# Stores of converted weight blocks moved from SyncE's DMA queue to ScalarE's, in an attention kernel followed by two feed-forward layers

## Chip, cores and metric

One core of one Trainium2 chip runs the whole program. The metric is the device time of one execution in microseconds (us); the time of a kernel is the median of its runs. A granted TensorE clock of 1.0 in a row is the 2.4 GHz level, 0.5 would be 1.2 GHz.

## What is computed

Pooled attention over 4 batches and 8 heads (q is averaged over pairs of neighbouring rows, so 576 query rows meet 1152 keys of 64 elements), then two feed-forward layers of 512 to 2048 to 512 on all 2304 rows, the first with a leaky ReLU, the second with an ELU.

```
q_pool = q.reshape(B, H, S // 2, 2, D).mean(axis=3)
scores = scale * q_pool @ k.T
attn   = softmax(scores)
x      = (attn @ v), heads side by side            # 2304 x 512
h = x @ w_in;  g = maximum(0.01 * h, h);           x = g @ w_out
h = x @ w_in2; g = where(h > 0, h, exp(min(h, 0)) - 1); out = g @ w_out2
```

q, k and v are float32. [...]

## The kernel before

**Matmuls.** Each float32 operand is split into a high part (rounded to the PE's float32r) and a low rest, and products are summed over two or three pairs of parts. The helper `psplit` (L261) records both steps: the rounding (L266 on ScalarE, called ACT below) and the subtraction (L272 on GpSimd, called POOL, or on VectorE, called DVE).

**Order of the work.** Nothing is issued where it is written. `prog.add` records an operation with its engine, an assumed cost, a rank (the smaller, the sooner) and the tiles it reads and writes; `Program.schedule` (L86) then plays all of it through with these costs, takes on each engine the ready operation of the lowest rank, and `emit` writes the instructions out in the order of the start times that come out. That order is fixed: on the chip each engine works through its own list and waits on semaphores. SyncE (SP) has no arithmetic; it issues DMAs, and each one in its list holds back those behind it while it waits. ACT computes and issues DMAs from the same list.

**Stages.** 16 pairs of heads (4 batches with 4 pairs each) go through attention. The feed-forward layers of a batch are woven into the attention of later batches by rank: `PLAN` (L219) starts layer 1 of batch 0 at rank 36 and its layer 2 at rank 54. Each layer takes the 2048 hidden elements in 16 blocks f of 128: `up` (L623) forms one block, and after every four blocks `down` (L662) sums them into the output.

**Weights.** `load_w` (L316) fetches for block f two pieces of 128 x 512, one of w_in and one of w_out, into two of four `wr` tiles. In batch 0 they are converted there by `convert` (L276): ACT issues the load of 512 KB of float64 into one of two `cr` tiles (L294), DVE makes the high bits (L297, L300), ACT scales the low word (L303) and takes the absolute value (L305), POOL adds (L308), and DVE clears the too small ones (L310). The block in `wr` is then stored to DRAM (L333, 256 KB, from SP's queue), and batches 1 to 3 read it back from there (L328, SP) without a conversion. In every batch the block goes from `wr` through `psplit` into `wi` or `wo` (rounding on ACT, subtraction on POOL). A `wr` tile can be overwritten once its rounding, its subtraction and its store are done.

**SP's other work.** In the same list stand the loads of q, k and v (L354), which use three `raw` tiles in turn; a load waits until POOL has finished with the tile. POOL splits k (L264, L272) and adds the pairs of rows of q (L402).

The lines that matter: L333, the store; L294, the loads that ACT issues already; L354, the loads of q, k and v on SP; L297 to L310, the conversion.

Of the kernel before, what the change touches and what calls it, by code (L numbers as in the profile page):

```python
# [157 lines left out]
def kernel(  # L158
# [19 lines left out]
    nc = tc.nc  # L178
# [59 lines left out]
    def f32(ap):  # L238
        return ap.bitcast(F32)
# [4 lines left out]
    prog = Program()  # L244

    def sb(tag, shape, dt=F32, bufs=1):
        return prog.buf(tag, bufs, lambda: sp.tile(shape, dt, tag=tag, name=tag, bufs=bufs))
# [4 lines left out]
    def act(n, accum=False, sbuf=False):  # L252
        return 50 + 0.833 * n + (190 if accum else 0) + (43 if sbuf else 0)

    def dve(n, fast=False):
        return 66 + (0.52 if fast else 1.05) * n

    def pool(n):
        return 140 + 2.12 * n

    def psplit(rank, h, l, hi, lo, src, n, w, r, w_l=None, fast=True, psum=False):  # L261

        if h == "POOL":
            prog.add("POOL", 100 + 1.1 * n, rank, lambda: G.tensor_copy(out=hi(), in_=src()), w=[w], r=r)  # L264
        elif h == "ACT":
            prog.add("ACT", act(n, sbuf=not psum), rank, lambda: A.activation(out=hi(), in_=src(), func=ACTF.Copy), w=[w], r=r)  # L266
        else:
            prog.add("DVE", dve(n, fast), rank, lambda: V.tensor_copy(out=hi(), in_=src()), w=[w], r=r)  # L268
        eng = V if l == "DVE" else G
        prog.add(  # L270
            l, dve(n) if l == "DVE" else pool(n), rank,
            lambda: eng.tensor_tensor(out=lo(), in0=src(), in1=f32(hi()), op=ALU.subtract),  # L272
            w=[w_l or (w[0], "l")], r=[w] + r)
# [42 lines left out]
    def load_w(rank, layer, w_in, w_out, f):  # L316

        src = (w_in[:, f * 128:(f + 1) * 128].rearrange("(c p) f -> p c f", p=128),
               w_out[f * 128:(f + 1) * 128, :])
        rs = [sb("wr", [128, 512], F32, WRB) for _ in range(2)]  # L320
        for i, r in enumerate(rs):
            if w_in.dtype == F32:
                view = (lambda r=r: r.ap.rearrange("p (c n) -> p c n", c=DC)) if i == 0 else lambda r=r: r.ap
                prog.add("SP", 60, rank - 1.5, lambda i=i, view=view: nc.sync.dma_start(
                    out=view(), in_=src[i]), w=[r])
            elif (layer, f, i) in kept:
                kp = kept[layer, f, i]
                prog.add("SP", 60, rank - 1.5, lambda r=r, kp=kp: nc.sync.dma_start(  # L328
                    out=r.ap, in_=kp.ap), w=[r], r=[kp])
            else:  # L330
                convert(rank - CLEAD, r, src[i])
                kp = kept[layer, f, i] = Buf(lambda i=i: dram.tile([128, 512], F32, name=f"w{layer}_{f}_{i}"))
                prog.add("SP", 60, rank, lambda r=r, kp=kp: nc.sync.dma_start(out=kp.ap, in_=r.ap), w=[kp], r=[r])  # L333
        wi = sb("wi", [128, 2, DC, 128], F32R, WIB)
        wo = sb("wo", [128, 2, DM], F32R, WOB)
        psplit(rank - 0.5, WH, WL, lambda: wi[:, 0].rearrange("p c n -> p (c n)"),
               lambda: wi[:, 1].rearrange("p c n -> p (c n)"), lambda: rs[0].ap, 512, (wi, 0), [rs[0]])
        psplit(rank - 0.5, WH, WL, lambda: wo[:, 0], lambda: wo[:, 1], lambda: rs[1].ap, 512, (wo, 0), [rs[1]])
        return wi, wo


# [258 lines left out]
    def mlp(at, span, b, layer, xin, w_in, w_out, tags):  # L600
# [22 lines left out]
        def up(f):  # L623
            rank = at + step * f
            w[f] = load_w(rank - WLEAD * step, layer, w_in, w_out, f)
            wi = w[f][0]
            g[f] = sb("g", [128, 2, NQ], F32R, GB)
# [108 lines left out]
    for b, layer, at, wide in PLAN:  # L736
        tags = [(u, size[u]) for u in ("h" * HBUFS + ("t" * TB + "s" * SBUFS if wide else ""))]
        w = ((moe_w_in, moe_w_out), (moe2_w_in, moe2_w_out))[layer]
# [35 lines left out]
```

## Time and profile before

| | |
|---|---|
| median of 3 runs | 1553.42 us (1551.05 to 1557.32) |
| the profiled execution, its own time | 1551.51 us |
| its span, first to last instruction | 1549.7 us |
| PE busy | 1416.1 us, 91% |
| ACT busy | 1017.4 us, 66% |
| DVE busy | 976.6 us, 63% |
| POOL busy | 874.8 us, 56% |
| stores of converted blocks | 64, from 35.3 to 581.7 us |
| float64 loads | 64, from 0.7 to 570.0 us |

Issuing a DMA does not count as busy; in the views of the trace such instructions stand under ACTq and SPq. "Idle before" an instruction is the idle time of its engine, and behind the arrow stands what ended it. Busy shares are means over the span; the stretch up to 585 us, in which weights are converted, is a different stage from the one behind it.

### The profile page before, as it was taken

To read this page: it belongs to the slowest core of one execution; us is meant where nothing else is said; L and a number is where in the kernel's file an instruction comes from. 1 tells how busy PE (TensorE), PEld (TensorE's weight loads), DVE (VectorE), ACT (ScalarE), POOL (GpSimd) and SP (SyncE) were. 2 spreads that over 40 slices of the span, in tenths; PEclk is the share of its full clock that TensorE was granted. 3 is DMA by queue.
4 is the path that set the end of the run, shared out by engine and by line. 5 is a ranking of instruction groups with operands and counts; after the bars stand their busy time and mean duration, and the time that the engine had idled before them with its cause. 6 is when DMAs were issued, how large, how long until landed. Compare 5 with 4: busy or idle time off the path is not lost.

```text
span 1549.7 us, 28278 instructions
## 1 busy us (share of the span) xinstructions
PE 1416.1 (91%) x10288; PEld 1359.9 (88%) x10288; DVE 976.6 (63%) x2081; ACT 1017.4 (66%) x2709; POOL 874.8 (56%) x840
## 2 busy tenths in 40 slices
PE   5878898889789988999999999999999998899998
PEld 4777788878778878999999999999999998898997
DVE  6999798788977887656665556656665554124122
ACT  5888777666677776666567776666567763442553
POOL 6544355756776686454565655454565445465562
PEclk9999999999999999999999999999999999999999
DMA  4332123424433432221222222221222111222221
GB/s 137 106 121 80 39 66 128 161 85 153 137 120 131 152 124 90 75 74 63 66 69 85 79 77 63 81 78 57 67 67 63 55 55 55 92 81 70 76 82 39
DMA packets 77516, 135.53 MB, mean 87 GB/s; under 512 B 7488, under 2 KB 25920, under 8 KB 77376
## 3 DMA queue, kind: packets, MB, share of 16 engines
q1 hardware_dynamic: 55872, 100.16, 20.6%
q10 hardware_dynamic: 21504, 33.56, 6.4%
q8 instruction: 81, 1.33, 0.4%
q14 instruction: 59, 0.48, 0.1%
HBM read 112.20 MB, written 21.50 MB: 86 GB/s over the span
## 4 chain that ended last, share of the span: by engine, by line
PE 51%; ACT 7%; DVE 6%; DMA 2%; issue 2%; POOL 1%; ACTq 0%; DVEq 0%; POOLq 0%
PE h L672 16%; PE h L634 12%; PE s L457 5%; PE o L501 4%; PE t L480 4%; PE s L634 3%; PE s L672 2%; PE t L672 2%; PE t L634 2%; ACT p L468 1%; DVE xs L268 1%; PE t L378 1%; ACT t L650 1%; DVE t L655 1%; DMA cr<-in_moe_w_in_dram 1%
## 5 line engine op out<-in xcount | busy, mean ns | idle before, releaser
L672 PE MATMUL h<-g,wo 128*128 128x288 f32 x2544 | 443.8, 304 | 22.5 <-DVE t L655 7.3
L634 PE MATMUL h<-xs,wi 128*128 128x288 f32 x2520 | 422.0, 303 | 21.4 <-DVE t L655 11.4
L672 PEld LDWEIGHTS h<-g,wo 128*128 128x128 f32 x2544 | 368.4, 189 | 30.1 <-DVE t L655 9.3
L634 PEld LDWEIGHTS h<-xs,wi 128*128 128x128 f32 x2520 | 357.2, 189 | 32.1 <-DVE t L655 17.7
L266 ACT ACTIVATE pt<-t 128x384 fp32r<-128x384 f32 (+1 forms) x416 | 185.3, 457 | 134.4 <-PE t L480 116.7
L462 DVE TENSOR_REDUCE m<-s 128x1 f32<-128x384 f32 x432 | 229.1, 550 | 68.2 <-PE s L457 65.6
L272 POOL TENSOR_TENSOR wo<-wr,wo 128x512 fp32r<-128x512 f32 x128 | 166.3, 1305 | 168.0 <-ACT wo L266 154.9
L468 ACT ACTIVATE p<-s,m 128x384 f32<-128x384 f32 x432 | 249.5, 587 | 15.9 <-DVE m L464 13.6
L272 POOL TENSOR_TENSOR g<-t,g 128x288 fp32r<-128x288 f32 x256 | 216.8, 853 | 75.4 <-ACT g L266 72.6
L272 DVE TENSOR_TENSOR pt<-t,pt 128x384 fp32r<-128x384 f32 (+1 forms) x416 | 206.5, 509 | 71.8 <-ACT pt L266 70.6
L457 PE MATMUL s<-kT,qT 128*128 128x384 f32 x768 | 194.5, 356 | 26.8 <-ACT p L468 25.3
L272 POOL TENSOR_TENSOR wi<-wr,wi 128x512 fp32r<-128x512 f32 x128 | 171.0, 1336 | 72.9 <-ACT wi L266 66.7
L501 PE MATMUL o<-pt,vn 128*128 128x256 f32 (+1 forms) x1152 | 191.1, 301 | 6.4 <-DVE pt L272 5.5
L480 PE MATMUL t<-ident,p 128*128 128x128 f32 x1116 | 181.8, 275 | 15.5 <-DVE pt L272 11.2
L501 PEld LDWEIGHTS o<-pt,vn 128*128 128x128 f32 x1152 | 164.4, 189 | 10.9 <-DVE pt L272 9.4
L480 PEld LDWEIGHTS t<-ident,p 128*128 128x128 f32 x1116 | 137.1, 141 | 27.1 <-DVE pt L272 14.0
L457 PEld LDWEIGHTS s<-kT,qT 128*128 128x128 f32 x768 | 126.3, 193 | 36.3 <-ACT p L468 33.2
L266 ACT ACTIVATE wo<-wr 128x512 fp32r<-128x512 f32 x128 | 80.8, 632 | 92.0 <-PE h L672 56.6
L266 ACT ACTIVATE g<-t 128x288 fp32r<-128x288 f32 x256 | 112.4, 447 | 34.7 <-DVE t L655 21.0
L264 POOL CAST vn<-raw 128x576 fp32r<-128x576 f32 x32 | 22.3, 696 | 181.2 <-PE o L501 181.2
L685 DVE TENSOR_TENSOR acc<-h,acc 128x288 f32<-128x288 f32 x158 | 70.8, 452 | 74.8 <-PE h L672 73.8
L308 POOL TENSOR_TENSOR wr<-wr,cr 128x512 uint32<-128x512 uint32 x64 | 88.9, 1393 | 33.6 <-DVE wr L300 16.7
(106 smaller groups left out, 2025.1 us busy)
## 6 DMA issues: line engine op xcount, KB each, us to landing
wr<-w SPq DMA_DIRECT2D x192, 256.0 KB, 2.6
cr<-in_moe_w_in_dram ACTq DMA_DIRECT2D x32, 512.0 KB, 4.0
cr<-in_moe_w_out_dram ACTq DMA_DIRECT2D x32, 512.0 KB, 4.3
w<-wr SPq DMA_DIRECT2D x64, 256.0 KB, 2.5
raw<-in_k_dram SPq DMA_DIRECT2D x32, 288.0 KB, 3.1
raw<-in_v_dram SPq DMA_DIRECT2D x32, 288.0 KB, 3.0
raw<-in_q_dram SPq DMA_DIRECT2D x32, 256.0 KB, 2.6
out_dram<-cr SPq DMA_DIRECT2D x16, 256.0 KB, 2.3
```

Of the source, the lines that this page charges most:

```text
L264: prog.add("POOL", 100 + 1.1 * n, rank, lambda: G.tensor_copy(out=hi(), in_=src()), w=[w], r=r)
L266: prog.add("ACT", act(n, sbuf=not psum), rank, lambda: A.activation(out=hi(), in_=src(), func=ACTF.Copy), w=[w], r=r)
L272: lambda: eng.tensor_tensor(out=lo(), in0=src(), in1=f32(hi()), op=ALU.subtract),
L308: prog.add("POOL", pool(CW), rank, lambda t=t, r=r: G.tensor_tensor(out=t(), in0=t(), in1=r[:, :, 0], op=ALU.add), w=[(dst, n)], r=[(dst, ...
L457: PE.matmul(out=st[:, 0:384], lhsT=qa(a), rhs=kT[:, 384 * c:384 * c + 384], start=(i == 0), stop=(i == len(seq) - 1))
L462: prog.add("DVE", dve(384), rank - LR, lambda st=st, c=c: V.tensor_reduce(out=m[:, c:c + 1], in_=st[:, 0:384], axis=AX.X, op=ALU.max), w=[ ...
L468: prog.add("ACT", act(384, True), rank - LE, lambda c=c: A.activation(out=p[:, 384 * c:384 * c + 384], in_=banks[c][:, 0:384], func=ACTF.E ...
L480: PE.transpose(out=t[:, i, :], in_=p[:, (3 * c + i) * 128:(3 * c + i + 1) * 128], identity=ident)
L501: PE.matmul(out=o[:, 0:n], lhsT=vn[:, c, :], rhs=pt[th][:, a, c % 3, :], start=(c == 3 * ORDER[0] and a == 0), stop=(c == 3 * ORDER[2] + 2 ...
L634: PE.matmul(out=h[:, 0:HB], lhsT=wi[:, a, c, :], rhs=xs[c][:, e, cols], start=(c == 0 and a == 0 and e == 0), stop=(c == DC - 1 and a == 1))
L672: PE.matmul(out=y[:, 0:HB], lhsT=w[f][1][:, a, d * 128:(d + 1) * 128], rhs=g[f][:, e, cols], start=(f % FC == 0 and a == 0 and e == 0), st ...
L685: prog.add("DVE", dve(HB), rank - HURRY, lambda y=y, a_=a_, cols=cols: V.tensor_tensor(out=a_[:, cols], in0=y[:, 0:HB], in1=a_[:, cols], o ...
```

## The change

The two stores of a block are no longer recorded for SP inside the loop that converts, but collected, and recorded for ACT after both roundings, with a rank 0.1 behind that of the roundings, an assumed cost of 80 ns, and an assumed 3000 ns until the data has landed. The line of the store is L342 in the changed kernel, and lines behind it are five higher.

```diff
         rs = [sb("wr", [128, 512], F32, WRB) for _ in range(2)]
+        stores = []
         for i, r in enumerate(rs):
...
                 convert(rank - CLEAD, r, src[i])
                 kp = kept[layer, f, i] = Buf(lambda i=i: dram.tile([128, 512], F32, name=f"w{layer}_{f}_{i}"))
-                prog.add("SP", 60, rank, lambda r=r, kp=kp: nc.sync.dma_start(out=kp.ap, in_=r.ap), w=[kp], r=[r])
+                stores.append((kp, r))
...
         psplit(rank - 0.5, WH, WL, lambda: wo[:, 0], lambda: wo[:, 1], lambda: rs[1].ap, 512, (wo, 0), [rs[1]])
+        for kp, r in stores:
+            prog.add("ACT", 80, rank - 0.4, lambda r=r, kp=kp: nc.scalar.dma_start(out=kp.ap, in_=r.ap), w=[kp], r=[r],
+                     late=3000)
         return wi, wo
```

What this makes of the lists is seen at three places. In a name, `w_11_0` is the store of block 11's piece of w_in, `w_11_1` that of w_out; `cr` loads are the float64 blocks. A bracket names the semaphores that an instruction waits on: DMAHW the completion of an earlier DMA, the others an engine's progress.

ACT, the conversion of blocks 11 and 12 of layer 1, before:

```order
L266 ACTIVATE pt<-t 128x3x128 [waits PE_49]
L294 DMA cr<-in_moe_w_in_dram 128x4x256 [waits DMAHW7_49,DVE_49]
L468 ACTIVATE p,sum<-s,m 128x384
L266 ACTIVATE pt<-t 128x3x128 [waits PE_49]
L423 ACTIVATE rem_73<-t 128x2x64 [waits PE_49]
L423 ACTIVATE rem_75<-t 128x2x64
L294 DMA cr<-in_moe_w_out_dram 128x1024 [waits DMAHW3_49,DVE_49,Activation_49]
L303 ACTIVATE cr<-cr 128x512 [waits DMAHW7_49]
```

and in the changed kernel:

```order
L266 ACTIVATE pt<-t 128x3x128 [waits PE_49]
L294 DMA cr<-in_moe_w_in_dram 128x4x256 [waits DVE_49]
L342 DMA w_11_0_3975<-wr 128x512 [waits DMAHW1_49]
L266 ACTIVATE pt<-t 128x3x128 [waits PE_49]
L294 DMA cr<-in_moe_w_out_dram 128x1024 [waits DVE_49,Activation_49]
L342 DMA w_11_1_4000<-wr 128x512 [waits DMAHW4_49]
L473 ACTIVATE p,sum<-s,m 128x384 [waits DVE_49]
```

A store now stands right behind a float64 load; none of the 64 waits on DVE itself, because an instruction ahead of it on ACT has waited for that already. Of the 64, 34 stand behind an ACTIVATE and 30 behind another DMA issue; 36 stand ahead of the rounding of their own block, which comes later in the list.

ACT, blocks 6 and 7 of layer 1, before:

```order
L294 DMA cr<-in_moe_w_in_dram 128x4x256
L266 ACTIVATE pt<-t 128x3x128
L682 ACTIVATE acc<-h 128x288
L266 ACTIVATE pt<-t 128x3x128
L294 DMA cr<-in_moe_w_out_dram 128x1024
L266 ACTIVATE pt<-t 128x3x128
```

and in the changed kernel:

```order
L294 DMA cr<-in_moe_w_in_dram 128x4x256
L266 ACTIVATE pt<-t 128x3x128
L687 ACTIVATE acc<-h 128x288
L266 ACTIVATE pt<-t 128x3x128
L342 DMA w_6_0_3191<-wr 128x512
L342 DMA w_6_1_3193<-wr 128x512
L342 DMA w_7_0_3195<-wr 128x512
L294 DMA cr<-in_moe_w_out_dram 128x1024
L266 ACTIVATE pt<-t 128x3x128
L342 DMA w_7_1_3214<-wr 128x512
```

Four stores have come together here, three of them ahead of a float64 load: the longest such run. From here to block 12 of layer 2 the order of PE, DVE and POOL differs too.

SP, around the end of layer 1's conversion, before:

```order
L333 DMA w_14_1_4543<-wr 128x512
L354 DMA raw<-in_v_dram 128x576
L333 DMA w_15_0_4634<-wr 128x512
L354 DMA raw<-in_k_dram 128x576
L354 DMA raw<-in_q_dram 128x512
L333 DMA w_15_1_4672<-wr 128x512
```

and in the changed kernel:

```order
L359 DMA raw<-in_v_dram 128x576
L359 DMA raw<-in_k_dram 128x576
L359 DMA raw<-in_q_dram 128x512
L359 DMA raw<-in_v_dram 128x576
L359 DMA raw<-in_k_dram 128x576
```

SP's list has lost the stores, and the loads of q, k and v follow each other in the same order as before.

## Rows read from the trace of the kernel before

**Rows 1.** The page: span, and busy time of the engines.

```profile
span 1549.7 us, 28278 instructions
PE 1416.1 (91%) x10288; PEld 1359.9 (88%) x10288; DVE 976.6 (63%) x2081; ACT 1017.4 (66%) x2709; POOL 874.8 (56%) x840
```

**Rows 2.** Busy time by stretch: length, PE, PEld, DVE, ACT, POOL, clock, DMA.

```profile
35.00:215.00 180.00, 148.46 (x1042) 135.66 (x1041) 162.43 (x372) 149.25 (x426) 81.53 (x78) 0.98 0.27 84
215.00:585.00 370.00, 320.16 (x2209) 295.61 (x2209) 305.47 (x573) 267.13 (x673) 252.55 (x214) 0.99 0.39 131
585.00:1550.00 965.00, 927.75 (x6930) 911.55 (x6929) 487.07 (x1096) 581.42 (x1562) 518.03 (x517) 1.00 0.22 70
```

**Rows 3.** The same view, the fullest and the emptiest 50 us while weights are converted.

```profile
250.00:300.00 50.00, 45.97 (x328) 43.59 (x327) 37.47 (x75) 38.36 (x98) 34.32 (x30) 0.97 0.35 118
400.00:450.00 50.00, 39.56 (x277) 36.69 (x276) 45.90 (x87) 33.59 (x84) 34.82 (x31) 0.99 0.35 116
```

**Rows 4.** The chain that ended last, 473 to 586 us, shares by line.

```profile
by line: DMA cr<-in_moe_w_in_dram 11.4%; DMA cr<-in_moe_w_out_dram 11.1%; issue 9.2%; DVE wr L297 7.1%; PE h L672 6.0%; DVE wr L310 5.9%; DVE wr L300 5.8%; PE h L634 5.8%; DVE m L462 4.2%; ACT p L468 3.9%; DVE t L655 2.9%; ACT cr L303 2.8%;
```

**Rows 5.** The stores on SP: waits (us, times, longest) and issue (ns min/median/max).

```profile
SPq L333 <- DVE wr L310: 318.8, 56, 13.9
L333 SPq DMA_DIRECT2D w<-wr x64: 319/321/337, 35.3 to 581.7; - x64
```

**Rows 6.** The float64 loads on ACT's queue: ns min/median/max, first and last start.

```profile
L294 ACTq EVENT_SEMAPHORE  x51: 17/17/2407, 32.9 to 567.8; - x51
L294 ACTq DMA_DIRECT2D cr<-in_moe_w_in_dram x32: 385/406/462, 0.7 to 567.9; - x32
L294 ACTq DMA_DIRECT2D cr<-in_moe_w_out_dram x32: 334/342/523, 1.2 to 570.0; - x32
```

**Rows 7.** ACT in order of time, around a single load: start us, us.

```profile
85.28 0.33 ACT L266 ACTIVATE pt<-h 128x192 fp32r<-128x192 f32 x1
85.37 0.33 ACTq L294 DMA_DIRECT2D cr<-in_moe_w_out_dram  x1
85.51 0.33 ACT L266 ACTIVATE pt<-h 128x192 fp32r<-128x192 f32 x1
```

**Rows 8.** ACT in order of time, around a pair of loads.

```profile
58.93 0.39 ACTq L294 DMA_DIRECT2D cr<-in_moe_w_in_dram  x1
59.43 0.44 ACTq L294 DMA_DIRECT2D cr<-in_moe_w_out_dram  x1
59.92 0.49 ACT L266 ACTIVATE pt<-t 128x384 fp32r<-128x384 f32 x1 [0.51 <-PE s L457]
```

**Rows 9.** ACT in order of time, a load issued at the end of an ACTIVATE.

```profile
534.66 0.39 ACTq L294 DMA_DIRECT2D cr<-in_moe_w_in_dram  x1
535.10 0.58 ACT L468 ACTIVATE p<-s,m 128x384 f32<-128x384 f32 x1 [0.41 <-DVE pt L272]
```

**Rows 10.** POOL's waits from 215 to 585 us: us, times, longest.

```profile
POOL qs L402 <- DMA raw<-in_q_dram: 13.5, 5, 3.7
```

**Rows 11.** Around 363 us in order of time: POOL, then SP, then DVE.

```profile
358.76 1.60 POOL L272 TENSOR_TENSOR kn<-raw,kn 128x576 fp32r<-128x576 f32 x1
...
367.80 0.77 POOL L402 TENSOR_TENSOR qs<-raw 128x256 f32<-128x256 f32 x1 [3.19 <-DMA raw<-in_q_dram]
368.54 1.30 POOL L308 TENSOR_TENSOR wr<-wr,cr 128x512 uint32<-128x512 uint32 x1
...
362.24 0.32 SPq L333 DMA_DIRECT2D w<-wr  x1
362.65 0.38 SPq L354 DMA_DIRECT2D raw<-in_k_dram  x1
363.14 0.39 SPq L354 DMA_DIRECT2D raw<-in_q_dram  x1
...
367.30 0.68 DVE L300 SCALAR_TENSOR_TENSOR wr<-cr,wr 128x512 uint32<-128x512 uint32 x1
...
370.02 0.68 DVE L310 SCALAR_TENSOR_TENSOR wr<-cr,wr 128x512 f32<-128x512 f32 x1
```

## Prediction, made before the changed kernel was run

> **What bounds the kernel now.** I began with the busy times of the page. PE is busy 1416.1 of 1549.7 us [rows 1], so all that a faster order could win is some 130 us of PE's idle time. The busy times by stretch say where that lies [rows 2]. From 585 us on, PE is busy 927.75 of 965 us, 96%: that part is bound by PE, holds no store, and keeps its order of instructions, so I carry it over as it is. From 215 to 585 us PE is busy 320.16 of 370 us, so 50 us are idle; from 35 to 215 us 148.46 of 180, so 32 us. The 64 stores run from 35.3 to 581.7 us [rows 5], in just these stretches. No engine is full in the longer one: DVE has 305.47 of 370 us, ACT 267.13, POOL 252.55. So the end is set by a chain that changes engines, and I read that next. Between 473 and 586 us the chain that ended last goes through the float64 loads (11.4 + 11.1%), the three DVE steps of the conversion (7.1 + 5.8 + 5.9%), and ACT's exponentials and scaling of low words (3.9 + 2.8%) [rows 4]. The stores are not named in it. What they can change is therefore how soon ACT gets through its list, since ACT issues the float64 loads, and how soon SP gets through its own.
>
> **Off SP.** SP loses 64 issues of 321 ns, and with them the waits in front of them: 318.8 us in 56 waits for L310 [rows 5]. SP computes nothing, so this counts only through the loads of q, k and v that stand behind a waiting store. Who is late because of them? From 215 to 585 us POOL waited five times for a q load, 13.5 us together [rows 10]. One of these places in full [rows 11]: POOL was done with the k tile at 358.76 + 1.60 = 360.36 us, but SP still held a store until 362.24, and issued k at 362.65 and q at 363.14. Without the store k could go at about 360.4, so q would land 2.3 us sooner and most of POOL's 3.19 us is gone. But what POOL does next, the addition L308 at 368.54, also needs L300 on DVE, which ended at 367.30 + 0.68 = 367.98. So L308 starts 0.56 us sooner at most, and DVE, which had other work until 370.02, need not notice. Bounds for this term: nothing, and all 13.5 us. I take **-1 us**, near the lower end, because this place, which is the row nearest to the question, gives at most 0.56 us and there are five of its kind.
>
> At this point the page "DMA: Bandwidth & Descriptors" of the Trainium skill (section "Issuing engines are not separate DMA queues") speaks against the change: all queues end on the same DMA engines, and issuing from another engine saves only issue time. By it this term would be 0 instead of -1. The 2.3 us of the place above disagree a little: what is saved there is a place in a list, not issue time.
>
> **Onto ACT: the issue.** Two kinds of issue on this queue last 406 and 342 ns [rows 6], and what one costs depends on what stands ahead of it. Behind an ACTIVATE, with nothing to wait for, it can be free: the load at 85.37 us was issued during the ACTIVATE from 85.28, and the next began at 85.51, before the issue was over [rows 7]. Of 25 loads that began to be issued before the ACTIVATE ahead had ended and have no other issue next to them, 18 read like this one and seven leave 2.8 us idle together; the one at 534.66, with 0.41, is of these [rows 9]. That is 2.8 / 25, about 0.1 us each. Behind another issue there is no cover: in the pair at 58.93 and 59.43 us the second left ACT idle for 0.51 us [rows 8], and I take 0.45, between its own 0.44 and that. With 34 stores of the first kind and 30 of the second the sum is 34 x 0.1 + 30 x 0.45 = 17 us of idle ACT. Bounds: 0, if all are covered, and 64 x 0.45 = 29 us.
>
> The page "Advanced Engine Details and Errata" (section "Sequencer and Instruction Queues") says that a sequencer pushes instructions ahead into a queue, eight deep on ScalarE, so that an issue runs beside them. By it the second kind could be covered as well and the 17 us would shrink to some 3; the 0.51 us of the pair go against it, and I go by them.
>
> How much of 17 us is on the path? In the chain the float64 loads and the two named ACT steps make up 11.4 + 11.1 + 3.9 + 2.8 = 29% [rows 4]; the loads come out of ACT's list, so they are late when it is. Not each of these pieces has a store ahead of it, so I take a quarter: **+4 us**. The bounds are 0 and the whole 29.
>
> **Onto ACT: the waits.** None of the stores waits for DVE; 44 of the 64 wait for an earlier DMA with the same completion semaphore, 22 of these for one of SP's. The nearest such DMA stands 14 ACT instructions earlier, and 14 at about half a microsecond are 7 us, longer than a transfer takes to land. So **0 us**. The bound above: the float64 loads carry the same kind of wait, and the longest time that this queue stood in one was 2407 ns while the median is 17 [rows 6]; a few of that length would stay below 10 us. Behind a store that waits stand the exponentials and the next float64 load, and for these wait the PE and the conversion.
>
> **Moved.** With the stores on ACT the planner brings other instructions out in another order between block 6 of layer 1 and block 12 of layer 2, about 245 to 580 us. Counted in the order of PE, blocks 4 to 11 of layer 1 start up to 27 matmuls of attention later, blocks 4 to 9 of layer 2 up to 17 earlier, and from block 12 on nothing differs. A `wr` tile is held until its store has landed, but between a store and the scaling for the next block in its tile stand at least 8 ACT instructions, nearly always over 15, so no new wait is expected there. The same work in a slightly other order has no sign that I can read: **0 us**. For the size, the fullest and the emptiest 50 us of this stage differ by 45.97 - 39.56 = 6.4 us of PE [rows 3], so I allow 6.4 us either way.
>
> **Sum.** -1 + 4 + 0 + 0 = +3 us. The profiled execution took 1551.5 us, which gives 1554.5; it lies 1.9 us below the median of the three runs (1553.4), so in terms of a median the forecast is **1556 us**, +0.2%. By a measurement of this kernel about 0.5%, 7.8 us, can be told from no change, so this is "no difference". Its own range is 1546 to 1561.
>
> **Rivals.**
> *Slower: ACT becomes the bound of the conversion.* Then the 17 us are not a quarter but wholly on the path. For it: from 35 to 215 us ACT is busy 149.25 of 180 us, 83%, without counting issues, and in the longer stretch each float64 load passes through its list. Against it: 9% of the chain is idle "issue" and most of the rest is DVE, DMA and PE [rows 4]. It gives 1551.5 + 17 - 1 + 1.9 = 1569, with the upper bound of 29 even 1581. It decides from 8 us on, a good half of the 17. Chance 0.22.
> *Faster: SP's list was the brake.* If each q load were in time and the stores were covered, 13.5 us of POOL's waiting would come back: 1551.5 - 13.5 + 1.9 = 1540. For it: the wait at 367.80 us stands right ahead of a conversion step on POOL [rows 11]. Against it: DVE's next step of that conversion began at 370.02, behind other work. Chance 0.15.
> *The other order decides.* It adds or takes 6.4 us: 1550 or 1563, the latter over the bound of 7.8 us, the former beyond it only if a term above ends at its low end too. What speaks for it is that two stretches of the same work differ by so much [rows 3], and against it that the list of PE is the same again from block 12 of layer 2 on. Chance 0.10, of which I count half as faster and half as slower.
> *The change doesn't do what it says.* The stores stand behind the roundings by rank only, and 36 come ahead of their own. But as none waits for DVE, this changes no time, and I leave it within the forecast.
>
> **How the numbers follow.** Forecast 0.53; slower 0.22 + 0.05 = 0.27; faster 0.15 + 0.05 = 0.20. The range that holds 8 in 10 reaches from 1542, which cuts off the deeper half of the faster case, to 1571, which holds the slower case at its 17 us and leaves out its upper bound.
>
> **What would show it.** Right: stores of about 0.35 us under ACTq, ACT's busy time unchanged at 1017 us, PE's busy time from 215 to 585 us the same within a few us, POOL's wait for q loads down from 13.5 us to under 6, and the stretch after 585 us unchanged in length. Wrong to the slow side: long waits under ACTq at L342, or a chain with ACT ahead of DVE. Wrong to the fast side: conversion ending well before 582 us and PE's idle time between 35 and 585 us well below the 82 us of now.

## The result: 15 us slower, and the profile after

The changed kernel takes 1567.57 us (median of 4 runs, 1565.01 to 1568.13) where the kernel before takes 1552.43 beside it (4 runs): ratio 1.0089, 95% interval 1.0063 to 1.0114. Timed once more, beside the hybrids below, it took 1564.91 us (6 runs, 1561.95 to 1566.78), ratio 1.0069 (1.0051 to 1.0087). So it is slower by 11 to 15 us, and both intervals lie over 0.5%. The execution shown here took 1567.23 us.

The page of the changed kernel, against [rows 1], and its busy times by stretch, against [rows 2]:

```profile
span 1565.5 us, 28217 instructions
PE 1425.3 (91%) x10288; PEld 1372.5 (88%) x10288; DVE 985.3 (63%) x2081; ACT 1020.6 (65%) x2709; POOL 873.7 (56%) x840
```

```profile
35.00:215.00 180.00, 147.86 (x1023) 135.70 (x1022) 160.35 (x367) 148.03 (x419) 79.82 (x76) 0.96 0.27 82
215.00:585.00 370.00, 317.07 (x2167) 294.99 (x2166) 305.11 (x556) 264.41 (x663) 247.69 (x213) 0.97 0.42 128
585.00:1550.00 965.00, 931.21 (x6921) 915.31 (x6920) 495.53 (x1112) 585.71 (x1573) 523.48 (x521) 0.99 0.24 70
```

ACT is no busier: 1020.6 us against 1017.4. But PE needs 9.2 us more for the same 10288 matmuls, and the granted clock is lower, most in the first two stretches (0.96 and 0.97, before 0.98 and 0.99). Fixed windows mislead where one kernel runs late, so I lined the two executions up by the number of matmuls done. At matmul 1344 (249.7 us before) the changed kernel is 1.7 us behind. There the orders part; at matmul 3732 (639.2 us before) it is 14.6 us behind, at the last one 15.7. Nearly all is lost between these two matmuls, so that is the stretch to look at. Here it is in the kernel before and, next, in the changed one (columns as in [rows 2]):

```profile
249.73:639.21 389.48, 341.81 (x2390) 318.60 (x2389) 310.62 (x601) 277.84 (x709) 259.37 (x224) 0.99 0.37 120
```

```profile
251.47:653.85 402.38, 347.61 (x2391) 326.79 (x2389) 320.81 (x602) 279.36 (x709) 257.99 (x224) 0.96 0.38 117
```

For the same matmuls (a row counts those at its edges too) PE is idle 402.38 - 347.61 = 54.8 us instead of 389.48 - 341.81 = 47.7, and busy 5.8 us longer, at a clock of 0.96 instead of 0.99. So 7 us are waiting, and 6 are matmuls that took longer.

Is it the stores on ACT? The view by line, for the stores and then for the first DVE step of a conversion (L297, which would wait if a `wr` tile were still held):

```profile
L342 ACTq DMA_DIRECT2D w<-wr x64: 326/456/905, 35.8 to 591.7; - x64
```

```profile
L297 DVE TENSOR_SCALAR wr<-cr x64: 408/742/1590, 5.9 to 584.9; 128x512 uint32<-128x512 uint32 x64
...
  DMA cr<-in_moe_w_in_dram: 10.4, 10
  DMA cr<-in_moe_w_out_dram: 5.2, 5
```

The issues last longer than on SP (median 456 ns against 321 [rows 5]), and the landing too (4.4 us against 2.5, medians), but of DMAs DVE's L297 waits for float64 loads alone, not for a store. Between the end of the ACT instruction ahead and the start of a store lie 0.6 us over all 64: the stores wait for nothing. ACT in order of time shows what the issues cost:

```profile
245.47 0.49 ACT L266 ACTIVATE pt<-t 128x384 fp32r<-128x384 f32 x1
245.55 0.43 ACTq L342 DMA_DIRECT2D w<-wr  x1
245.86 0.40 ACT L687 ACTIVATE acc<-h 128x288 f32<-128x288 f32 x1
246.01 0.46 ACTq L342 DMA_DIRECT2D w<-wr  x1
246.15 0.50 ACT L266 ACTIVATE pt<-t 128x384 fp32r<-128x384 f32 x1
246.50 0.51 ACTq L342 DMA_DIRECT2D w<-wr  x1
248.16 0.34 ACTq L294 DMA_DIRECT2D cr<-in_moe_w_out_dram  x1
248.55 0.49 ACT L266 ACTIVATE pt<-t 128x384 fp32r<-128x384 f32 x1 [1.90 <-DVE m L467]
```

The three ACTIVATEs follow without a gap, and the first two of three stores are issued beside them. The third is covered for 0.15 of its 0.51 us only; behind it ACT stands idle, 1.90 us in all, of which 1.15 lie between the end of this issue and the start of the next load's. Over all 64 stores, the part of the issues that no ACT instruction covers is 10.9 us of 29.3.

### The profile page after: what moved, and what is told of

Its sections match the earlier page's. It is cut to its first block, busy times and chain, and to the rows that moved or that the text cites. A ratio compares the mean times of both kernels' runs of the same rounds, so it can differ in the third digit from the quotient of the medians.

```text
span 1565.5 us, 28217 instructions
## 1 busy us (share of the span) xinstructions
PE 1425.3 (91%) x10288; PEld 1372.5 (88%) x10288; DVE 985.3 (63%) x2081; ACT 1020.6 (65%) x2709; POOL 873.7 (56%) x840
## 3 DMA queue, kind: packets, MB, share of 16 engines
q8 instruction: 81, 1.33, 0.3%
## 4 chain that ended last, share of the span: by engine, by line
PE 60%; DVE 14%; ACT 10%; DMA 7%; issue 5%; POOL 3%; ACTq 0%; SPq 0%; POOLq 0%; DVEq 0%
PE h L677 15%; PE h L639 13%; PE s L462 8%; PE o L506 7%; PE t L485 5%; DMA cr<-in_moe_w_out_dram 4%; PE s L639 3%; PE s L677 2%; ACT pt L266 2%; DVE wr L310 2%; ACT p L473 2%; DVE m L467 2%; PE t L677 2%; PE t L639 2%; DVE wr L300 2%
## 5 line engine op out<-in xcount | busy, mean ns | idle before, releaser
L639 PEld LDWEIGHTS h<-xs,wi 128*128 128x128 f32 x2520 | 360.9, 191 | 32.4 <-DVE t L660 15.3
L506 PEld LDWEIGHTS o<-pt,vn 128*128 128x128 f32 x1152 | 164.5, 189 | 10.9 <-DVE pt L272 9.6
L485 PEld LDWEIGHTS t<-ident,p 128*128 128x128 f32 x1116 | 138.4, 141 | 26.0 <-DVE pt L272 12.5
L266 ACT ACTIVATE wo<-wr 128x512 fp32r<-128x512 f32 x128 | 81.0, 633 | 85.8 <-PE h L677 54.8
L690 DVE TENSOR_TENSOR acc<-h,acc 128x288 f32<-128x288 f32 x158 | 71.0, 452 | 77.0 <-PE h L677 75.8
```

The costliest lines, as they stand in the source:

```text
L485: PE.transpose(out=t[:, i, :], in_=p[:, (3 * c + i) * 128:(3 * c + i + 1) * 128], identity=ident)
L506: PE.matmul(out=o[:, 0:n], lhsT=vn[:, c, :], rhs=pt[th][:, a, c % 3, :], start=(c == 3 * ORDER[0] and a == 0), stop=(c == 3 * ORDER[2] + 2 ...
L639: PE.matmul(out=h[:, 0:HB], lhsT=wi[:, a, c, :], rhs=xs[c][:, e, cols], start=(c == 0 and a == 0 and e == 0), stop=(c == DC - 1 and a == 1))
L690: prog.add("DVE", dve(HB), rank - HURRY, lambda y=y, a_=a_, cols=cols: V.tensor_tensor(out=a_[:, cols], in0=y[:, 0:HB], in1=a_[:, cols], o ...
```

## Experiments: the queue or the order

Three theories. **Issue**: the stores take time in ACT's list. **Hold**: they land later there and hold `wr` tiles. **Order**: the planner, told of another engine and other costs, brings all other instructions out in another order, and that is worse. The first two runs take the change apart: one has the changed order with the stores on SP, the other the old order with the stores on ACT.

**sp_new_order**

```diff
-            prog.add("ACT", 80, rank - 0.4, lambda r=r, kp=kp: nc.scalar.dma_start(out=kp.ap, in_=r.ap), w=[kp], r=[r],
+            prog.add("ACT", 80, rank - 0.4, lambda r=r, kp=kp: nc.sync.dma_start(out=kp.ap, in_=r.ap), w=[kp], r=[r],
```

> The changed kernel's lists on every engine, instruction by instruction, but each store issued from SP at the place where the changed kernel issues it from ACT. Theory 'order' (the 15 us come from the other order of PE, DVE, POOL and ACT between block 6 of layer 1 and block 12 of layer 2): 1567 us, within 4. Theory 'issue' (they come from the stores' issues and waits in ACT's list): back to 1553, within 4. Theory 'hold' (they come from the later landing on ACT's queue, 4.4 us against 2.5): 1553 as well, with the landing back at 2.5 us.

Measured: 1562.39 us (6 runs), ratio 1.0059 (1.0043 to 1.0076). With the stores back on SP the loads of q wait behind them again: POOL waits 12.5 us for them from 215 to 585 us, about as before (13.5 [rows 10]), and 2.9 in the changed kernel.

**act_old_order** (against the kernel before; the planner still books the store on SP)

```diff
-        for i in sorted(range(len(start)), key=lambda i: (start[i], i)):
+        for i in sorted(range(len(start)), key=lambda i: (start[i] + self.defer.get(i, 0), i)):
...
+                prog.defer[len(prog.ops)] = 3000
-                prog.add("SP", 60, rank, lambda r=r, kp=kp: nc.sync.dma_start(out=kp.ap, in_=r.ap), w=[kp], r=[r])
+                prog.add("SP", 60, rank, lambda r=r, kp=kp: nc.scalar.dma_start(out=kp.ap, in_=r.ap), w=[kp], r=[r])
```

> The lists of the kernel before on every engine; each store is planned as before, but issued from ACT, 3 us of the plan later, so that ACT does not stand waiting for DVE (one store of 64 does). Theory 'order': 1553 us, within 4. Theory 'issue': 1567, within 4, most of it already lost between 250 and 620 us. Theory 'hold': 1567 too, with longer waits of DVE at the first step of a conversion for the store's landing, which 'issue' does not need.

Measured: 1551.66 us (12 runs), ratio 0.9992 (0.998 to 1.0003). POOL's waits for q loads are down to 1.5 us. Nearly all issues lie beside an ACT instruction here: 1.7 of 21.9 us are uncovered, against 10.9 in the changed kernel.

**act_old_behind_rounding**: as the last, but each store is issued by the function that issues the rounding of its own block.

```diff
-            prog.add("ACT", act(n, sbuf=not psum), rank, lambda: A.activation(out=hi(), in_=src(), func=ACTF.Copy), w=[w], r=r)
+            prog.add("ACT", act(n, sbuf=not psum), rank, lambda: (A.activation(out=hi(), in_=src(), func=ACTF.Copy), then and then()), w=[w], r=r)
```

> The lists of the kernel before, each store issued from ACT directly behind the rounding of its own block, so later than in the changed kernel, and its wr tile held longer. Theory 'order': 1553 us, within 4. Theory 'issue': 1567, within 4. Theory 'hold': slower than the run with the stores 3 us later, 1570 or more, and DVE waits for a store's landing at the first step of a conversion.

Measured: 1553.58 us (12 runs), ratio 0.9998 (0.9985 to 1.0012). Here the view of L297 does name the store:

```profile
  DMA w<-wr: 5.7, 4
```

**act_no_late**: the changed kernel without `late=3000`.

```diff
-            prog.add("ACT", 80, rank - 0.4, lambda r=r, kp=kp: nc.scalar.dma_start(out=kp.ap, in_=r.ap), w=[kp], r=[r],
-                     late=3000)
+            prog.add("ACT", 80, rank - 0.4, lambda r=r, kp=kp: nc.scalar.dma_start(out=kp.ap, in_=r.ap), w=[kp], r=[r])
```

> The changed kernel with the planner's 3000 ns until the landing taken out: stores still on ACT, again another order from the same stretch on. Theory 'order': some other time, between 1545 and 1575, over 4 us away from 1567.6 more likely than not. Theory 'issue': 1567, within 4, since ACT issues the same 64 stores. Theory 'hold': within 4 of 1567 or above, as the planner now takes tiles again before the store has landed.

Measured: 1554.68 us (12 runs), ratio 1.001 (0.9998 to 1.0022).

What follows. "Hold" falls: with the old order nothing is lost, even where four tiles are waited for, 5.7 us. "Issue" falls as the cause of the 15 us: with the old order and the issues covered nothing is lost, and `act_no_late` has the stores on ACT in pairs as the changed kernel has (12.0 us of them uncovered) and loses 3.4 us at most by its interval. A part of that size isn't excluded. "Order" stands: with the stores on SP the changed order loses 9 us. That POOL waits for q there explains little of it, since before it waited as long, and `act_old_order`, without these waits, is no faster that one could tell. The PE list of `act_no_late` differs from that of before in 1037 of 10288 places (the changed kernel's in 1125). So it isn't that the order differs, but which one it is. The same matmuls as above in these runs, first `sp_new_order`, then `act_old_order`, then `act_no_late`:

```profile
249.12:647.11 397.99, 343.44 (x2391) 323.51 (x2390) 317.79 (x602) 278.75 (x709) 256.40 (x224) 0.97 0.36 117
```

```profile
251.19:642.86 391.67, 342.84 (x2391) 321.38 (x2390) 312.06 (x600) 277.73 (x709) 259.70 (x224) 0.98 0.39 120
```

```profile
249.59:638.46 388.87, 341.27 (x2391) 321.97 (x2390) 313.40 (x601) 278.38 (x709) 259.58 (x224) 0.97 0.40 121
```

PE's idle time is 54.6 us with the changed order on SP (54.8 on ACT), and 48.8 and 47.6 in the other two (47.7 before). It goes with the order and not with the queue. What remains between `sp_new_order` and the changed kernel is not idle time but PE's busy time, 343.44 against 347.61 us, at a clock of 0.97 against 0.96. The mean clock alone doesn't give the busy time, though: `act_no_late`, at 0.97 as well, has 341.27. More of the clock below.

One place shows what such an order does. PE in order of time, the same group of up-block matmuls (24 for one bank) in the kernel before, the changed kernel and `sp_new_order`:

```profile
380.65 3.70 PE L634 MATMUL h<-xs,wi 128*128 128x288 f32 x24
384.18 0.51 PE L457 MATMUL s<-kT,qT 128*128 128x384 f32 x2
```

```profile
385.50 0.56 PE L639 MATMUL h<-xs,wi 128*128 128x288 f32 x3
387.22 3.07 PE L639 MATMUL h<-xs,wi 128*128 128x288 f32 x21 [1.16 <-DVE acc L690]
390.12 0.82 PE L485 MATMUL t<-ident,p 128*128 128x128 f32 x6
392.23 2.65 PE L639 MATMUL h<-xs,wi 128*128 128x288 f32 x18 [1.29 <-DVE t L652]
```

```profile
383.10 3.05 PE L639 MATMUL h<-xs,wi 128*128 128x288 f32 x21 [1.17 <-DVE acc L690]
385.99 0.82 PE L485 MATMUL t<-ident,p 128*128 128x128 f32 x6
387.97 2.65 PE L639 MATMUL h<-xs,wi 128*128 128x288 f32 x18 [1.16 <-DVE t L652]
```

Before, the first 24 run without a stop. In both kernels with the changed order PE stops twice, by 1.16 to 1.29 us, for a step of DVE that reads a bank out. DVE at this place in the kernel before, and in the changed one:

```profile
378.57 0.71 DVE L310 SCALAR_TENSOR_TENSOR wr<-cr,wr 128x512 f32<-128x512 f32 x1
379.70 0.56 DVE L462 TENSOR_REDUCE m<-s 128x1 f32<-128x384 f32 x1 [0.41 <-PE s L457]
380.32 0.43 DVE L514 TENSOR_TENSOR xu<-o,tm 64x256 f32<-64x256 f32 x1
380.78 0.46 DVE L685 TENSOR_TENSOR acc<-h,acc 128x288 f32<-128x288 f32 x1
```

```profile
384.88 1.33 DVE L310 SCALAR_TENSOR_TENSOR wr<-cr,wr 128x512 f32<-128x512 f32 x1
386.25 0.43 DVE L519 TENSOR_TENSOR xu<-o,tm 64x256 f32<-64x256 f32 x1
386.71 0.46 DVE L690 TENSOR_TENSOR acc<-h,acc 128x288 f32<-128x288 f32 x1
391.71 0.46 DVE L652 TENSOR_TENSOR t<-h,t 128x288 f32<-128x288 f32 x1 [3.52 <-ACT t L650]
```

The first stop: before, L310, the last step of a conversion, ended 1.5 us ahead of the sum L685, with two other steps between. In the changed order it comes later, lasts 1.33 us (why, these rows don't show) and stands with L519 right ahead of the sum (L690 here), for which PE waits.

The second stop has another origin: DVE's L652 itself waits for ACT, where L650 stands behind the scaling L303 of a low word. L303 in the kernel before, the changed one and `sp_new_order`:

```profile
383.50 0.67 ACT L303 ACTIVATE cr<-cr 128x512 uint32<-128x512 uint32 x1 [1.99 <-DMA cr<-in_moe_w_out_dram]
```

```profile
390.73 0.65 ACT L303 ACTIVATE cr<-cr 128x512 uint32<-128x512 uint32 x1 [3.47 <-DMA w<-wr]
```

```profile
386.47 0.66 ACT L303 ACTIVATE cr<-cr 128x512 uint32<-128x512 uint32 x1 [3.31 <-DMA cr<-in_moe_w_out_dram]
```

The view of the changed kernel names a store as what ended this wait. But the wait is about as long in `sp_new_order`, where no store is on ACT and the float64 load is named. So both stops come with the stores on either queue.

## Experiments: is it one place?

**after_again** is the changed kernel, unaltered; its time stands above.

> The changed kernel itself once more, beside the hybrids: 1567, within 3. If it lies at 1562, the order alone (1562.4 with the stores on SP) is the whole loss; if at 1567 again, about 5 us need the stores on ACT as well.

Its time lies between the two that were expected, at 1564.91, and the two intervals (1.0051 to 1.0087, and 1.0043 to 1.0076 for `sp_new_order`) overlap.

**new_until_368** and **old_until_368** play both plans through and change from one to the other; the first is shown, in the second the two are exchanged and the cut is 303100. The cut is in the plan's time and falls at matmul 2077. **no_late_until_471** does the same with the plan of `act_no_late`, cut at 379400.

```diff
-        start = self.schedule()
-        for i in sorted(range(len(start)), key=lambda i: (start[i], i)):
+        new = self.schedule()
...
+        old = self.schedule()
...
+        for i in sorted(range(len(new)), key=lambda i: (
+                (0, place["new"][i], i) if new[i] < 303200 else (1, place["old"][i], i))):
```

> Stores on ACT; the changed kernel's order up to matmul 2077 (368 us in the trace of before), from there on the order of before. Theory 'order, place by place': each stretch keeps its own loss; up to matmul 2061 the changed kernel lost 3.5 us and the old order behind it loses nothing, so 1553 to 1557. Theory 'first slip' (the early difference delays the conversion, and everything behind is late for it, whatever the order there): 1562 or more.

Measured: 1556.96 us (12 runs), ratio 1.0021 (1.0007 to 1.0036).

> Stores on ACT; the order of before up to matmul 2077, then the changed kernel's order. Theory 'order, place by place': the changed kernel lost 11 us behind matmul 2061, so 1560 to 1566. Theory 'first slip': 1553 to 1557, since the early difference is gone.

Measured: 1560.14 us (7 runs), ratio 1.0045 (1.0027 to 1.0062).

> Stores on ACT; up to matmul 2660 (471 us in the trace of before) the order of the kernel without the planner's 3000 ns, which was 6.8 us ahead of before there (2 us less idle PE, 4.6 us less at the low clock), then the order of before. Theory 'order, place by place': part of that lead stays, 1546 to 1550, faster than both. If the lead was that execution's clock alone, or is given back behind the cut: 1552 to 1555.

Measured: 1550.77 us (12 runs), ratio 0.9989 (0.9973 to 1.0006).

The two halves cost 0.21% and 0.45%, together 0.66%, and the whole order 0.69% in the same comparison: the loss adds up over the two halves, and "first slip" falls, since it gave 1562 or more with the old order behind the cut, and no loss with the changed order behind it. The third is not settled: by the medians 2.3 of the 6.8 us are kept, and the interval holds 1. So no version here beats the kernel before.

## Experiments: what ACT does mind, and the planner's number

**act_old_double**: `act_old_order` with each store issued twice.

```diff
+                prog.add("SP", 60, rank, lambda r=r, kp=kp, k2=k2: (
+                    nc.scalar.dma_start(out=kp.ap, in_=r.ap), nc.scalar.dma_start(out=k2.ap, in_=r.ap)), w=[kp], r=[r])
```

> The old order with the stores on ACT, and each store issued twice in a row from ACT, the second to a DRAM tile that nothing reads. If issues on ACT are off the path here, within 4 us of the run with one (1551.7). If a quarter of the idle ACT behind them is on it, as the prediction had it: 64 second issues x 0.45 = 29 us, so 1559. If all of it: 1580.

Measured: 1555.87 us (12 runs), ratio 1.0016 (1.0002 to 1.003), against 0.9992 with one. 64 issues more, all right behind another issue, cost 4.2 us, just over the limit set for "off the path" (2.5 us, if it is compared with the kernel before): 0.07 us each, about a seventh of the 0.45 that I had taken as idle ACT, and not far from the quarter of that, 0.11, which I had put on the path. 11.5 us of the issues are uncovered here, as many as in the changed kernel (10.9). So some 2.5 to 4 us of the changed kernel's loss may be its issues; no run settles it.

**act_unshifted**: `act_old_order` without the 3 us.

```diff
-                prog.defer[len(prog.ops)] = 3000
```

> The old order, each store issued from ACT at the very place in the plan where SP had it, that is as soon as the plan has DVE finish the block: now the store is the first of ACT's list to wait for that DVE step. If ACT seldom reaches it early: 1553 to 1557. If waits at the head of ACT's list bite: each holds up exponentials and float64 loads; a microsecond in half of the 64 would be 32 us of waiting, a quarter of it on the path 8, so 1560 or more, with the waits under ACTq at the store.

Measured: 1564.12 us (4 runs), ratio 1.0063 (1.0044 to 1.0082). 24 stores now start over 0.3 us behind the instruction ahead on ACT, 20.6 us together. The longest, ACT and then DVE in order of time:

```profile
409.90 0.68 ACT L305 ACTIVATE cr<-cr 128x512 f32<-128x512 f32 x1
412.91 0.33 ACTq L333 DMA_DIRECT2D w<-wr  x1
413.36 0.39 ACTq L294 DMA_DIRECT2D cr<-in_moe_w_in_dram  x1
```

```profile
411.09 1.79 DVE L310 SCALAR_TENSOR_TENSOR wr<-cr,wr 128x512 f32<-128x512 f32 x1
```

ACT is done at 410.58 and stands for 2.3 us until L310 ends at 412.88, with a float64 load behind the store. So 20.6 us of waiting on ACT (in the profiled execution, the slowest of the four) go with 12.5 us against the same lists with the store 3 us later (1564.12 - 1551.66; 11 by the ratios), while the issues alone, 21.9 us in `act_old_order`, cost nothing that can be told. What made ACT's queue free to use there is that the stores stood behind something that had already waited.

**late_4500** and **late_6000**: the changed kernel with another number.

```diff
-                     late=3000)
+                     late=4500)
```

> The changed kernel with 4500 ns instead of 3000 assumed until the landing; stores on ACT. Theory 'the planner holds the wr tiles too long' (its assumed landing pushes the next conversion back, and the more the longer): 1568 or more. Theory 'any other order, with no rule': anywhere between 1547 and 1570.

Measured: 1565.93 us (4 runs), ratio 1.008 (1.0063 to 1.0097).

> The same with 6000 ns. 'The planner holds the tiles too long': slower than with 4500, 1570 or more. 'No rule': anywhere between 1547 and 1570, and not in the order of the assumed times.

Measured: 1560.34 us (4 runs), ratio 1.0043 (1.0027 to 1.0059).

With 0, 3000, 4500 and 6000 ns the ratios are 1.001, 1.0069 to 1.0089, 1.008 and 1.0043. The longest assumption is not the slowest, so "the planner holds the tiles too long" is not the rule. All three orders with a `late` lose and the one without doesn't; why, I did not find. The same matmuls as above, in `late_4500` and `late_6000`:

```profile
252.00:651.97 399.97, 343.55 (x2391) 320.08 (x2390) 323.24 (x602) 276.96 (x709) 261.39 (x224) 0.98 0.38 118
```

```profile
251.01:648.24 397.23, 343.61 (x2391) 318.38 (x2390) 319.07 (x602) 277.69 (x709) 259.73 (x224) 0.99 0.38 118
```

PE is idle 56.4 and 53.6 us in them, as in the changed order (54.8), against 47.6 to 48.8 in the kernel before, `act_old_order` and `act_no_late`. In `late_6000` the clock is that of before, 0.99, and 5.9 of the 7.8 us that the stretch is longer are idle time: the order costs time without the lower clock too.

## Why the prediction was right or wrong

The time came 11.6 us over the forecast of 1556 (8.9 when it was timed again), and over the forecast's own range, which ended at 1561. It lies inside the range that was to hold 8 in 10, up to 1571, but only because a rival with another mechanism had stretched that; this is luck. By the steps:

- **Off SP, -1 us: right, as far as can be told.** POOL's waits for q loads fell from 13.5 us in five [rows 10] to 2.9 in three in the changed kernel, and to 1.5 in two in `act_old_order`, whose time didn't fall by anything that can be told (0.9992, 0.998 to 1.0003). The Trainium skill's rule (page "DMA: Bandwidth & Descriptors", section "Issuing engines are not separate DMA queues") that another issuing engine saves only issue time gave 0. The runs allow that as well; they can't tell 0 from -1.
- **Onto ACT, the issue, +4 us: idle ACT too large, the time on the path not refuted.** I expected 17 us of idle ACT, and 10.9 us of issue lie uncovered. Behind another issue I took 0.45 us for each, from one pair [rows 8]; but that row names PE, not the issue, as what ended the idle time, and at 245 us one of two such issues is fully covered. On the path is nothing where the issues are covered (`act_old_order`), and where as much is uncovered as here it is 2.5 to 4 us (`act_old_double`) or nothing to 3.4 (`act_no_late`). The Trainium skill's page "Advanced Engine Details and Errata" (section "Sequencer and Instruction Queues") lets an issue run beside queued instructions, and by it some 3 us would be left. The first two stores at 245 us agree with that, the third lies mostly beside an idle ACT; the 10.9 us are about halfway between that and my 17.
- **Onto ACT, the waits, 0 us: right**, 0.6 us over 64 stores. `act_unshifted` shows that the worry was just: there, with waits of 20.6 us, 11 to 12.5 are lost.
- **The `wr` tiles: right.** No wait of DVE's L297 for a store's landing in the changed kernel, although it landed 1.9 us later.
- **Moved order, "0 us", with 6.4 us either way: this step failed.** I wrote that the same work in another order has no sign that I can read. It had one, and a size that the term put at nothing: about +9 us by `sp_new_order`, +0.66%, some 10 us, by the sum of the hybrids. The allowance was too small as well, because it was made of PE's idle time in 50 us alone: the idle time that the order added, 7 us, is about that size, but the lower clock that came with it was in no term.
- **The stretch behind:** from matmul 3732 to the last the difference grew by 1.1 us, as expected nearly nothing.

The rival "ACT becomes the bound" gave 1569, close to the time, by the wrong mechanism: where the old order stays, the issues on ACT cost 4.2 us even with twice as many (`act_old_double`). The rival with the true mechanism, "the other order decides", gave 1563 at most. What spoke against it, that PE's list is the same again from block 12 of layer 2 on, is no argument: the time lost by then stays lost. And the signs that I named for the slow side, long waits at L342 or a chain with ACT ahead, did not appear. Those for "right" did in part: ACT's busy time, PE's from 215 to 585 us (317.07 against 320.16) and POOL's waits came out as named, so none of these signs tells a worse order apart.

**Left open.** The changed kernel is 2.5 to 5 us above `sp_new_order`, with the same idle PE. In the profiled executions it goes with a lower clock, and the clock of the changed kernel differs between executions: of its ten, one at a mean of 0.994 took 1561.95 us, one at 0.984 took 1568.13. Whether the ACT queue shifts the idle times so that the clock falls more often there, whether the uncovered issues cost it (2.5 to 4 us by `act_old_double`), or whether these few runs differ by chance, these runs don't settle. Nor was an order tried that keeps only L310 behind L690.

## What to carry to other kernels

Where a planner sets the order, moving one instruction to another engine is two changes: the queue and the order of everything else. Separate them before you explain, by building the new order with the old queue and the old order with the new queue. An issue on a busy compute engine was nearly free here as long as something ahead of it had waited already; a wait at the head of that engine's list was not.

## What the runs showed of the hardware

**A short wait of PE can be paid twice.** Busy times of the changed kernel around one place, and of the same place when it was run again (columns as in [rows 2]):

```profile
448.00:455.50 7.50, 4.39 (x29) 3.53 (x26) 6.79 (x11) 5.29 (x14) 6.81 (x6) 0.88 0.18 51
455.50:462.50 7.00, 7.00 (x36) 7.00 (x37) 3.87 (x8) 5.19 (x16) 5.86 (x5) 0.64 0.72 209
462.50:470.00 7.50, 5.53 (x40) 5.07 (x40) 6.90 (x12) 6.37 (x16) 5.58 (x6) 1.00 0.24 75
```

```profile
448.00:455.50 7.50, 4.14 (x25) 3.28 (x24) 6.95 (x11) 5.30 (x14) 6.82 (x5) 0.87 0.17 45
455.50:462.50 7.00, 7.00 (x37) 7.00 (x38) 3.79 (x9) 5.12 (x15) 5.94 (x6) 0.65 0.73 194
```

PE is busy 4.39 of 7.5 us; then the granted clock is 0.64 on average, part of it at the 1.2 GHz level, and PE is busy all the time with 36 matmuls, where the next stretch does 40 in 5.53 us at 1.00. So an idle time of 3.1 us is followed by some 2 us of slow matmuls (an estimate from these rows: 36 at the later rate would take 5.0 us), just when there is work again. Both executions fall at the same place, so where the clock falls goes, at least here, with where the order of the work leaves PE idle. The order doesn't fix all of it: with one and the same PE list the whole stretch had a clock of 0.99 in the kernel before and 0.98 in `act_old_order`.

**The time of one kernel goes with its clock from execution to execution.** Of 29 runs of the kernel before, the four with a mean clock of 0.994 or above took 1549.7 to 1552.9 us, and the three at 0.988 took 1556.6 to 1559.8. It is a tendency, not a rule: of 17 others the three at 0.988 took 1552.9 to 1558.0. A median of four runs still has some of that in it.
